# A fused attention and routing kernel on one core: new start, new ending, and three sets of transposes moved from TensorE to the DMA queues

## The chip, the core and the metric

The kernel runs on one core of one Trainium2 chip. A core has five instruction streams that run side by side and meet only at semaphores: PE (TensorE, the matrix multiplier, which writes to PSUM), ACT (ScalarE), DVE (VectorE), POOL (GpSimd) and SP (SyncE, which here only issues DMAs). Each stream executes its instructions strictly in the order in which they were written. The metric is the device time of one execution in microseconds; lower is better. Three runs of the kernel before are given, and one execution was recorded by the profiler.

## The reference, cut to what matters

The input is 2048 tokens of 512 bf16 values. They are normalized (xn), then two branches read xn, and their outputs are added to x.

```python
xn = layernorm(x)
# branch A: 32 heads of 16, four segments of 512 tokens, per segment s:
q, k, v = heads(xn @ wq), heads(xn @ wk), heads(xn @ wv)
phi = lambda t: where(t > 0, t + 1, exp(t))
a_dot = softmax(qs @ ks.T * scale + causal_mask) @ vs
a_mem = (phi(qs) @ M) / (phi(qs) @ z + 1e-6)          # M, z from earlier segments
o     = g * a_mem + (1 - g) * a_dot                   # g = sigmoid(beta)
M, z  = M + phi(ks).T @ vs, z + phi(ks).sum(0)
A = o @ wo
# branch B: one token is chosen and sent through a gated MLP
r = xn @ w_r;  t = argmax(r)
y = (silu(xn[t] @ w_gate) * (xn[t] @ w_up)) @ w_down * sigmoid(r[t])
B = xn, with y added to row t
out = x + A + B
```

Three things must be transposed on the way, since a matrix product on PE contracts over the partitions: xn (tokens on partitions, needed with channels on partitions), phi(K) (needed with tokens on partitions for `phi(ks).T @ vs`) and the attention output O (tokens on partitions, needed with channels on partitions for `o @ wo`).

## The kernel before

All work is cut into operations that are put on record through `Plan.op`: an engine, an assumed duration, what it reads and writes, and a due time `d`. `Plan.run` (L75) then simulates the engines with these durations and writes the instructions in the order that this gives: of the operations that could start, the one with the earliest due time goes first. The order on every engine is thus fixed when the program is built. The due times, and a field `e` before which the planner doesn't place an operation, exist only in the planner: on the chip an instruction starts when its engine reaches it and its semaphores are there.

The main loop is over 16 groups n: segment s = n // 4 and eight heads j = n % 4 of it. Each group has two units of four heads, and each unit five tiles of causal attention scores, so there are 160 tiles. A tile (`tile`, L426) is: PE computes scores into a PSUM buffer `st` (L436), ACT takes their exponential into `pt` (L439), POOL zeroes the part above the diagonal (L448), and PE multiplies with V into the accumulator `acc` (L457, 8 small products). There are two `st` buffers, two `acc` buffers and two further PSUM buffers, called `misc`, for everything else that PE computes. After the five tiles DVE divides by the row sums (L422, L423) and writes `Oseg`.

Around the tiles, PE has other work that the planner puts in between:

- the projections of K, Q and V (L358, L400), 512 columns each product;
- `ln` for the tokens of the next segment: DVE takes the statistics (L305), POOL normalizes (L321), PE transposes four 128x128 blocks into `misc` (L331), and DVE copies them to `xnT` (L334);
- `phi` (L366 to L369) of K and, from segment 1 on, of Q;
- `memT` (L463): PE transposes phi(K), four blocks at a time (L469), and DVE copies them to `pk` (L471); `memM` multiplies with V (L482), and `mem` applies the memory of earlier segments to phi(Q) (L505, L509), after which POOL adds the result to `Oseg` (L520);
- `fin` (L537), once for each block of 128 tokens: PE transposes four blocks of `Oseg` (L545), DVE copies them to `oT` (L547), PE adds a row block `rb` made by POOL (L525) and the product with `wo` (L550, L552), DVE adds x times a scale (L532), SP stores the block;
- `oT3` (L555): the same transposes for the last segment, kept in a buffer of their own;
- `moe` (branch B) and `guard` (a check of the norms of wq and wk, L574 to L598, whose result decides at L962 whether a slow path is run; it isn't run with these inputs).

SP issues all transfers, in the planned order: the loads, eight small DMAs for each group that place Q's heads into the zeroed buffers `QZ` (`scatter`, L373), and the stores. A DMA takes one of eight semaphores in turn, and waits until the DMA that had it before has landed.

The start: SP loads four blocks of x, then wk, wq, wv; PE runs 14 products on zeros; POOL clears `QZ` and sets `Vaug`'s ones; DVE normalizes four blocks; PE transposes them; K and Q of group 0 are projected from all four blocks at once, and four heads of `QZ` are written straight from PSUM by DVE and ACT (L811, L813). The ending (L850 to L880): the final products of four token blocks are started in two `misc` buffers and one `st` buffer (L859, L861), the last eight heads' part is transposed on PE together with the memory part (L866, L867), multiplied (L875), and DVE makes the four output blocks in turn (L878), which SP stores.

## Time and profile before

| what | value |
|---|---|
| median of 3 runs (lowest, highest) | 231.29 us (229.43, 232.02) |
| the profiled execution | 231.71 us |
| its span, first to last instruction | 230.0 us |
| mean granted TensorE clock | 0.95 |
| busy: PE, ACT, DVE, POOL | 204.0, 172.3, 158.2, 151.7 us |
| DMAs of Q's heads, count and size | 124 of 16 KB |

The profile is a recording of one execution. Its span is 1.71 us shorter than the time of that execution, which also counts what lies outside the first and last instruction. A busy time is the union of an engine's instructions; for PE, where the end of a product is modelled, it is better to compare the starts of neighbouring rows.

### The profile page before, as it was taken

Reading aid. Unit: us, or ns where it says so; the run is one execution under the profiler, and the core shown is the slowest. Engines: PE = TensorE matmul, PEld = TensorE weight load, DVE = VectorE, ACT = ScalarE, POOL = GpSimd, SP = SyncE. Lnnn points to the kernel's source line nnn. Section 1 sums busy time; section 2 is a strip of 40 time slices with the busy share of each in tenths; the row PEclk is TensorE's granted clock in tenths of the full one; section 3 lists DMA queues with packets and bytes.
Section 4 is the critical chain, followed back from the end, with each engine's and each line's share of the span. In section 5 each row is a group of like instructions: output and inputs, shape, how many; then the busy total and the mean of one; then the engine's idle time right before and its main releaser. Section 6 shows DMA issues by size and latency. Waiting matters only on the chain.

```text
span 230.0 us, 6827 instructions
## 1 busy us (share of the span) xinstructions
PE 204.0 (89%) x2680; PEld 133.5 (58%) x2717; DVE 158.2 (69%) x392; ACT 172.3 (75%) x203; POOL 151.7 (66%) x252
## 2 busy tenths in 40 slices
PE   7386999989999999989999999999989999998720
PEld 2143656656677677755677666556557767676410
DVE  6966999664776964554677977897787966583060
ACT  3127899999988968987687879968567998889300
POOL 8802487976965664847477689999627578868400
PEclk9769999999999988988999999999999999999965
DMA  5800597031000012660000010010100001110020
GB/s 172 273 13 7 155 297 261 24 102 23 4 6 22 3 27 58 234 215 12 14 4 24 24 43 29 30 44 26 46 1 28 20 17 36 36 37 26 0 95 15
DMA packets 15195, 14.39 MB, mean 63 GB/s; under 512 B 3184, under 2 KB 15152, under 8 KB 15152
## 3 DMA queue, kind: packets, MB, share of 16 engines
q1 hardware_dynamic: 15152, 13.85, 19.5%
q8 instruction: 23, 0.38, 0.7%
q14 instruction: 20, 0.16, 0.2%
HBM read 9.71 MB, written 2.10 MB: 51 GB/s over the span
## 4 chain that ended last, share of the span: by engine, by line
PE 55%; DVE 20%; ACT 7%; issue 5%; DMA 5%; POOL 4%; SPq 1%; POOLq 0%; ACTq 0%
PE st L436 19%; PE misc L358 9%; PE acc L457 8%; ACT pt L439 6%; PE misc L552 4%; PE misc L400 4%; DVE bnst L305 3%; DMA x_all<-in_A_x_dram 3%; POOL pt L448 2%; DMA QZ<-raw_q 2%; DVE KT L390 2%; DVE Oseg L423 1%; PE misc L550 1%; DVE ob L532 1%; PE misc L331 1%
## 5 line engine op out<-in xcount | busy, mean ns | idle before, releaser
L439 ACT ACTIVATE pt<-st 128x1024 bf16<-128x1024 f32 x160 | 155.2, 1025 | 30.3 <-PE st L436 24.5
L448 POOL TENSOR_SCALAR_AFFINE_SELECT pt<-pt 128x512 bf16<-128x512 bf16 (+1 forms) x160 | 88.1, 556 | 54.0 <-ACT pt L439 51.4
L436 PE MATMUL st<-QZ,KT 128*128 128x512 bf16 (+3 forms) x507 | 95.8, 302 | 3.3 <-DVE QZ L811 1.2
L457 PEld LDWEIGHTS <-pt 128*128 128x128 bf16 x1280 | 50.0, 96 | 22.7 <-POOL pt L448 6.5
L457 PE MATMUL acc<-Vaug,pt 128*128 128x17 bf16 x1280 | 53.5, 171 | 2.8 <-POOL pt L448 1.5
L436 PEld LDWEIGHTS <-KT 128*128 128x128 bf16 x512 | 39.1, 98 | 17.1 <-issue 5.8
L358 PE MATMUL misc<-xnT,wk 128*128 128x512 bf16 x57 | 18.4, 406 | 1.2 <-ACT xnT L336 0.7
L367 POOL TENSOR_SCALAR am<-ex 128x512 bf16<-128x512 bf16 x24 | 14.9, 622 | 6.8 <-ACT ex L366 6.2
L358 PE MATMUL misc<-xnT,wq 128*128 128x512 bf16 x55 | 17.3, 395 | 0.5 <-issue 0.2
L400 PE MATMUL misc<-wv,xnT 128*128 128x512 bf16 x58 | 16.6, 378 | 1.0 <-DVE raw_q L815 0.6
L520 POOL TENSOR_TENSOR Oseg<-Oseg,om 128x512 bf16<-128x512 bf16 x11 | 13.4, 1219 | 3.5 <-DVE om L515 2.1
L532 DVE SCALAR_TENSOR_TENSOR ob<-x_all,s,misc 128x512 bf16<-128x512 bf16 x12 | 9.0, 747 | 9.2 <-PE misc L552 9.0
L422 DVE RECIPROCAL rr<-acc 128x16 f32<-128x16 f32 x32 | 7.9, 247 | 9.8 <-PE acc L457 9.8
L402 DVE TENSOR_TENSOR Vaug<-misc,omg_bc 128x512 bf16<-128x512 f32 x16 | 11.0, 689 | 4.6 <-PE misc L400 4.3
L423 DVE TENSOR_TENSOR Oseg<-acc,rr 128x256 bf16<-128x256 f32 x32 | 13.5, 423 | 0.9
L379 DVE CAST raw_q<-misc 128x512 bf16<-128x512 f32 x15 | 10.3, 688 | 5.5 <-PE misc L358 3.0
L525 POOL TENSOR_SCALAR rb<-ybc,onehot,cvec 128x512 bf16<-128x512 bf16 x16 | 12.3, 771 | 0.8 <-DVE rm L511 0.3
L390 DVE CAST KT<-misc 128x512 bf16<-128x512 f32 x15 | 10.3, 687 | 3.5 <-PE misc L358 2.8
L305 DVE BATCH_NORM_STATS2 bnst<-x_all 128x6 f32<-128x512 bf16 x16 | 10.7, 670 | 0.9 <-DMA x_all<-in_A_x_dram 0.9
L552 PE MATMUL misc<-wo,oT 128*128 128x512 bf16 x40 | 10.7, 378 | 0.4
L331 PE MATMUL misc<-ident,xn 128*128 128x128 bf16 x64 | 6.8, 240 | 4.3 <-DVE xn L321 2.9
L358 PEld LDWEIGHTS <-wk 128*128 128x128 bf16 x64 | 6.0, 100 | 6.2 <-issue 1.8
(154 smaller groups left out, 258.4 us busy)
## 6 DMA issues: line engine op xcount, KB each, us to landing
out_dram<-ob SPq DMA_DIRECT2D x16, 128.0 KB, 1.8
QZ<-raw_q SPq DMA_DIRECT2D x124, 16.0 KB, 1.8
mw<-in_B_w_gate_dram SPq DMA_DIRECT2D x2, 896.0 KB, 7.0
mw<-in_B_w_up_dram SPq DMA_DIRECT2D x2, 896.0 KB, 6.6
mw<-in_B_w_down_dram SPq DMA_DIRECT2D x2, 896.0 KB, 5.9
x_all<-in_A_x_dram SPq DMA_DIRECT2D x3, 512.0 KB, 4.4
x_all<-in_A_x_dram SPq DMA_DIRECT2D x4, 128.0 KB, 2.2
wk<-in_A_wk_dram SPq DMA_DIRECT2D x1, 512.0 KB, 4.2
```

The lines of the kernel that those rows point to most:

```text
L305: pl.op("DVE", .61, lambda: nc.vector.bn_stats(out=st[:], in_=x_all[:, b, :]), r=[("x", b)], w=[st], d=d)
L358: self.pl.op("PE", .216, lambda cb=cb: nc.tensor.matmul(ps[:], lhsT=w[:, cb, j * P:(j + 1) * P], rhs=xnT[:, cb, s * L:(s + 1) * L], start= ...
L367: pl.op("POOL", .58, lambda: nc.gpsimd.tensor_scalar(out=am[:], in0=ex[:], scalar1=1.0, scalar2=0.0, op0=ALU.min, op1=ALU.max), r=[ex], w= ...
L390: o = self.pl.op("DVE", .61, lambda: nc.vector.tensor_copy(out=kt[:], in_=ps[:]), r=[ps], w=[kt], d=d + 1)
L400: self.pl.op("PE", .216, lambda cb=cb: nc.tensor.matmul(ps[:], lhsT=xnT[:, cb, b * P:(b + 1) * P], rhs=wv[:, cb, :], start=(cb == 0), stop ...
L423: pl.op("DVE", .345, lambda: nc.vector.tensor_tensor(out=Oseg[s][:, j, :, 4 * w:4 * w + 4, :], in0=av()[:, :, :, 0:DH], in1=rr[:, :, :, No ...
L436: nc.tensor.matmul(st[:, i, off:off + n], lhsT=lh, rhs=QZ[q][:, h, q0:q0 + n], start=True, stop=True)
L439: pl.op("ACT", .907, lambda: nc.scalar.activation(out=pt[:], in_=st[:], func=ACT.Exp, scale=SCALE), r=[st], w=[pt], d=d)
L448: nc.gpsimd.affine_select(out=mv, in_=mv, pattern=pat, compare_op=ALU.is_ge, fill=0.0, base=0, channel_multiplier=-1)
L457: nc.tensor.matmul(acc[:, q0 // P + c, i, e, :], lhsT=pt[:, i, off + c * P:off + (c + 1) * P], rhs=Vaug[:, 4 * s + kb, h, :], start=first, ...
L520: pl.op("POOL", 1.12, lambda: nc.gpsimd.tensor_tensor(out=Oseg[s][:, j], in0=Oseg[s][:, j], in1=om[:], op=ALU.add), r=[om], w=[("O", s, j, ...
L552: pl.op("PE", .216, lambda cb=cb: nc.tensor.matmul(fin[:], lhsT=oT[:, cb, :], rhs=wo[:, cb, :], start=False, stop=(cb == NCB - 1)), r=[oT, ...
```

## The change

The change has four parts.

**Transposes by DMA.** The transposes of xn for segments 1 to 3 (12), of phi(K) (12, now cut by heads j and not by token block) and of O (12 in `fin`, 4 in `oT3`) become `dma_start(..., transpose=True)` on SP's queue, 128x512 bf16 each (128x256 in `oT3`). They write SBUF, so the `misc` buffer and DVE's copy go away. `Oseg` is laid out by token block first, so that a block's 512 columns are contiguous.

**The start.** x's blocks 1 and 3 and wk are loaded from ACT's queue. POOL's and DVE's clearing is put in another order, constants that are used late are set later, 22 products on zeros are spread among the transposes, the projections of group 0 go block by block, K is copied by ACT, and all four heads of `QZ` come from the bf16 copy `raw0`. The four transposes of the first segment stay on PE.

**The ending.** O's transposes for the heads j = 2 and 3 of the last segment stay on PE and take the memory part with them (`late`). Two of the four final blocks get x times its scale from PE, through three bf16 diagonal matrices whose sum is the scale to f32 precision (L904 of the changed kernel), and go out through ACT, copy and DMA.

**The planner.** Scores, exponentials and the products with V are kept in the order of the tiles; an operation of DVE that is marked `lock` is planned at times at which POOL is idle; `moe` is due 5 earlier and its small products are spread out; `guard` multiplies the other way round, so that each sum has one column and not 512.

```diff
         def ln_T(self, b, xb, eng, d):
             pl = self.pl
+            if eng == "DMA":
+                pl.op("SP", .5, lambda: nc.sync.dma_start(out=xnT[:, :, b * P:(b + 1) * P], in_=xb[:], transpose=True), r=[xb], w=[("xnT", b)], d=d, lat=DTL)
+                return
...
-            self.pl.op("PE", .226, mm, r=[("pkT", s, j) for j in range(NCB)], uses=[src], w=[tp], d=d)
-            o = self.pl.op("DVE", .33, lambda: nc.vector.tensor_copy(out=pk[:, tb, :], in_=tp[:].rearrange("p j c -> p (j c)")), r=[tp], w=[("pk", s, tb)], uses=[pk], d=d + .5)
+            self.pl.op("SP", .5, lambda: nc.sync.dma_start(out=pk[:, :, j * P:(j + 1) * P], in_=src[:, j, :], transpose=True), r=[("pkT", s, j)], w=[("pk", s, j)], uses=[src, pk], d=d, lat=DTL)
...
-            pl.op("PE", .226, mm, r=[("O", s, j, w) for j in range(NCB) for w in range(2)], w=[ops], d=d)
-            o = pl.op("DVE", .33, lambda: nc.vector.tensor_copy(out=oT[:], in_=ops[:]), r=[ops], w=[oT], d=d + .5)
+            pl.op("SP", .5, lambda: nc.sync.dma_start(out=oT[:], in_=Oseg[s][:, qb].rearrange("p c a b -> p (c a b)"), transpose=True), r=[("O", s, j, w) for j in range(NCB) for w in range(2)], w=[oT], d=d - 2, lat=DTL)
...
-                    pl.op("PE", .216, lambda sq=sq, ps=ps: nc.tensor.matmul(ps[:], lhsT=ones_colb[:], rhs=sq[:], start=True, stop=True), r=[sq], w=[ps], d=dd + 1)
+                        for j in range(NCB):
+                            nc.tensor.matmul(ps[:, j:j + 1], lhsT=sq[:, j * P:(j + 1) * P], rhs=ones_colb[:], start=True, stop=True)
...
+    for b in (0, 2):
+        ld("SP", [("x", b)], x_all[:, b, :], x_d[:, b, :], .1 * b, 2.1)
+        ld("ACT", [("x", b + 1)], x_all[:, b + 1, :], x_d[:, b + 1, :], .1 * b, 2.1)
+    ld("SP", ["wq"], wq[:], wap(A_wq), 1.0, 4.5)
+    ld("ACT", ["wk"], wk[:], wap(A_wk), 1.1, 4.5)
...
+            for tb in range(4):
+                for t, w, wkey, dd in ((psq, wq, "wq", 8.0), (ps, wk, "wk", 8.1)):
...
+            pl.op("DVE", .61, lambda: nc.vector.tensor_copy(out=raw0[:], in_=psq[:]), r=[psq], w=[raw0], d=8.5)
+            pl.op("ACT", .6, lambda: nc.scalar.copy(out=kt0[:], in_=ps[:, 0, :]), r=[ps], w=[kt0], d=9)
+            for i, h in enumerate((0, 2, 1, 3)):
+                pl.op("DVE", .22, lambda h=h: nc.vector.tensor_scalar(out=QZ[0][:, h, :], in0=raw0[:], scalar1=bdsel[:, h:h + 1], scalar2=None, op0=ALU.mult), r=[raw0], w=[("QZ", 0, h)], d=9 + .1 * i, lock=True)
...
+            pl.op("DVE", 1.0, diag, r=[("s1", bb), "cpool"], w=dg + [res], d=td(150), lock=True)
+            for i in range(3):
+                pl.op("PE", .216, lambda t=t, i=i, dg=dg, bb=bb, sub=sub: nc.tensor.matmul(sub(t), lhsT=dg[i][:], rhs=x_all[:, bb, :], start=False, stop=False), r=[dg[i]], w=[key], uses=[t], d=dd)
...
-        pl.op("SP", .5, lambda b=b, tt=tt: nc.sync.dma_start(out=out_d[:, b, :], in_=tt[:]), r=[tt], d=td(165))
+        if qb >= 2:
+            pl.op("DVE", .66, lambda b=b, t=t, tt=tt, sub=sub: nc.vector.scalar_tensor_tensor(out=tt[:], in0=x_all[:, b, :], scalar=s1[:, b:b + 1], in1=sub(t), op0=ALU.mult, op1=ALU.add),
+                  r=[key, ("s1", b)], w=[tt], uses=[t], d=td(164))
+        else:
+            pl.op("ACT", .6, lambda t=t, tt=tt, sub=sub: nc.scalar.copy(out=tt[:], in_=sub(t)), r=[key], w=[tt], uses=[t], d=td(164))
+        eng = "SP" if qb >= 2 else "ACT"
```

How it moves instructions, at three places. The first is POOL's row from the late constants on to the first work of group 0, before (`QZ_145` and `QZ_146` are the two Q buffers, `sq` belongs to `guard`, `am` to phi):

```order
L255 IOTA tokidx 128x16
L770 MEMSET QZ_145 128x1024
L774 MEMSET Vaug 128x128
L772 MEMSET QZ_146 128x1024 x4
L774 MEMSET Vaug 128x128 x3
L574 TENSOR_TENSOR sq<-wq 128x512 x2
L367 TENSOR_SCALAR am<-ex 128x512
L448 AFFINE_SELECT pt<-pt 128x2x128
```

and now, where the Q buffers are `QZ_136` and `QZ_137`:

```order
L776 MEMSET QZ_136 128x1024
L234 AFFINE_SELECT bdsel<-bdsel 128x8
L778 MEMSET Vaug 128x128
L776 MEMSET QZ_137 128x1024
L454 AFFINE_SELECT pt<-pt 128x2x128
L776 MEMSET QZ_137 128x1024
L454 AFFINE_SELECT pt<-pt 128x2x256
L454 AFFINE_SELECT pt<-pt 128x4x128
```

Before, nine clearings and two squarings stood ahead of everything that waits for another engine; now the masks of the first tiles come after four clearings (one more of `QZ_136` stands a few rows above), and the rest is spread among them.

The second is SP's row in the third segment, where the stores of segment 1 go out, before:

```order
L534 DMA out_dram<-ob 128x512 x2
L373 DMA QZ_145<-raw_q 16x512 x8
L534 DMA out_dram<-ob 128x512 x2
L373 DMA QZ_146<-raw_q 16x512 x8
L534 DMA out_dram<-ob 128x512 x2
```

and now (`Oseg_141` is segment 1's output, `pkT` is phi(K)):

```order
L541 DMA_TRANSPOSE oT<-Oseg_141 128x4x128 x2
L533 DMA out_dram<-ob 128x512
L379 DMA QZ_136<-raw_q 16x512 x5
L471 DMA_TRANSPOSE pk<-pkT 128x4x128
L379 DMA QZ_136<-raw_q 16x512 x3
L471 DMA_TRANSPOSE pk<-pkT 128x4x128
L533 DMA out_dram<-ob 128x512
L471 DMA_TRANSPOSE pk<-pkT 128x4x128
L533 DMA out_dram<-ob 128x512
L541 DMA_TRANSPOSE oT<-Oseg_142 128x4x128 x2
L379 DMA QZ_137<-raw_q 16x512 x8
```

The transposes stand between the eight DMAs of a group and ahead of those of the next.

The third is PE's row at the last tile, before (`st<-wo,oT_153` belongs to the final products in the `st` buffer, `st<-QZ_146,KT` is the last tile's score):

```order
L861 LDWEIGHTS oT_153
L861 MATMUL st<-wo,oT_153 128x512
L436 LDWEIGHTS KT
L436 MATMUL st<-QZ_146,KT 128x512
L436 LDWEIGHTS KT
L436 MATMUL st<-QZ_146,KT 128x512
L457 LDWEIGHTS pt
L457 MATMUL acc<-Vaug,pt 128x17
```

and now, behind the 24 products with V that follow that score:

```order
L463 LDWEIGHTS pt
L463 MATMUL acc<-Vaug,pt 128x17
L890 LDWEIGHTS ident
L890 MATMUL st<-rb,ident 128x512
L906 LDWEIGHTS oT_144
L906 MATMUL st<-wo,oT_144 128x512
```

The final products that use the `st` buffer stood ahead of the last tile's score, and now stand behind it.

More of the change, by code (lines that the diff above doesn't have):

```diff
@@ L146, in run @@
             free[e] = end
+            if o["lock"]:
+                port[0] = end
             fin = end + o["lat"]
@@ L261, in build_kernel @@
     xnT = big.tile([P, NCB, S], bf16, name="xnT")
-    Oseg = [big.tile([P, NCB, 4, 8, DH], bf16, name=f"Oseg{s}") for s in range(NSEG)]
+    Oseg = [big.tile([P, 4, NCB, 8, DH], bf16, name=f"Oseg{s}") for s in range(NSEG)]
     oT3 = big.tile([P, 4, NCB, P], bf16, name="oT3")
@@ L599, in guard @@
-            pl.op("DVE", .5, last, r=[("fs", 0), ("fs", 1)], w=["nbad"], d=d + 28)
+                            nc.vector.tensor_tensor(out=sqs[:, i, :], in0=sqs[:, i, :], in1=ps[:], op=ALU.add)
+                    self.misc.append(pl.op("DVE", .1, acc, r=[ps, ("sqs", i)], w=[("sqs", i)], d=dd + 2))
+            nbad_i = small_t["nbad"] = stat.tile([1, 1], i32, name="nbad_i")
+            hs, bad, cnt = stat.tile([8, 2, NCB], f32, name="hs"), stat.tile([8, 3], f32, name="bad"), self.ps([1, 1])
@@ L847, in build_kernel, with late, mm @@
     pl.op("SP", .3, values, r=["nbad"], d=td(152), e=td(120))
+    def late(j, ts, d):
+        for hb in range(2):
+            for qb in (2 * hb, 2 * hb + 1):
+                def mm(hb=hb, qb=qb):
+                    nc.tensor.matmul(ts[hb][:, qb % 2, :], lhsT=Oseg[3][:, qb, j].rearrange("p a b -> p (a b)"), rhs=ident[:], start=True, stop=False)
+                    nc.tensor.matmul(ts[hb][:, qb % 2, :], lhsT=B.om_late[j][:, qb].rearrange("p a b -> p (a b)"), rhs=ident[:], start=False, stop=True)
+                pl.op("PE", .115, mm, r=[("O", 3, j, 0), ("O", 3, j, 1), B.om_late[j]], w=[ts[hb]], d=d)
+            if hb == 0 or j == 2:
+                o = pl.op("DVE", .3, lambda hb=hb: nc.vector.tensor_copy(out=oT3[:, 2 * hb:2 * hb + 2, j, :], in_=ts[hb][:]), r=[ts[hb]], w=[("oT3l", j, hb)], d=d)
+            else:
+                o = pl.op("ACT", .35, lambda hb=hb: nc.scalar.copy(out=oT3[:, 2 * hb:2 * hb + 2, j, :], in_=ts[hb][:]), r=[ts[hb]], w=[("oT3l", j, hb)], d=d)
+            if j == 2:
+                B.misc.append(o)
+    late(2, [B.ps([P, 2, P]) for i in range(2)], td(152.5))
     busy = list(B.misc)
```

304 lines of the change are left out of this document (151 added, 153 removed).

## The prediction

> **What bounds the kernel now.** I read the busy time by stretches first, then who waits for whom, then PE's own rows in order of time, then the start and the ending. The first view has, for each stretch, its length and the busy time of PE, PE's weight loads, DVE, ACT and POOL with the number of instructions, then granted clock and DMA share:
>
> ```profile
> 19.60:60.00 40.40, 38.05 (x487) 24.48 (x494) 31.25 (x76) 38.49 (x49) 29.47 (x50) 1.00 0.40 124
> 60.00:100.00 40.00, 39.26 (x690) 28.59 (x696) 26.73 (x84) 34.67 (x41) 26.01 (x44) 0.96 0.20 60
> 100.00:140.00 40.00, 38.51 (x510) 25.81 (x517) 28.94 (x71) 31.17 (x37) 27.41 (x45) 0.96 0.14 43
> 140.00:180.00 40.00, 38.15 (x441) 23.83 (x448) 31.46 (x68) 29.88 (x34) 31.09 (x47) 1.00 0.09 26
> 180.00:213.00 33.00, 31.91 (x454) 22.41 (x459) 22.09 (x56) 30.32 (x34) 24.53 (x42) 1.00 0.10 29
> ACT pt L439 <- PE st L436: 24.5, 30, 3.4
> ```
>
> The first tiles are bound by ACT (38.5 of 40.4 us). From 60 us on ACT is busy for 126 of 153 us and PE for 147.8. The last row says whom ACT waits for: PE's scores, 24.5 us in all. So from 60 us on the sum of PE's work sets the pace. That PE has work without a gap, and isn't just shown busy, is read from its starts:
>
> ```profile
> 138.77 0.38 PE L575 MATMUL misc<-sq,ones_colb 128*1 128x512 bf16 x1
> 139.08 0.40 PE L545 MATMUL misc<-ident,Oseg 128*128 128x128 bf16 x4
> 139.32 1.18 PE L436 MATMUL st<-QZ,KT 128*128 128x512 bf16 x4
> 92.22 0.84 PE L695 MATMUL misc<-xselT,mw 128*128 128x1 bf16 x28
> 92.92 0.59 PE L436 MATMUL st<-QZ,KT 128*128 128x512 bf16 x2
> ```
>
> Each row starts where the one ahead of it lets go: four transposes (L545) take 0.24 us of PE, one product of `guard` 0.31, and 28 products of one column 0.70, or 0.025 each.
>
> **The start.** In order of time (start, duration, engine, line; in brackets the idle time before and what ended it):
>
> ```profile
> 0.80 1.28 ACT L221 ACT_TABLE_LOAD   x1 [0.80 <-PEq L1002]
> 0.80 2.10 DMA x_all<-in_A_x_dram
> 2.92 0.69 DVE L305 BATCH_NORM_STATS2 bnst<-x_all 128x6 f32<-128x512 bf16 x1 [0.76 <-DMA x_all<-in_A_x_dram]
> 3.23 3.93 POOL L772 MEMSET QZ<- 128x1024 bf16 x4
> 6.11 0.18 DVE L306 BATCH_NORM_AGGREGATE MV<-bnst 128x2 f32<-128x6 f32 x1
> 6.21 3.80 DVE L321 TENSOR_SCALAR xn<-x_all,rstd,cvec 128x512 bf16<-128x512 bf16 x2
> 9.92 0.99 DVE L315 SCALAR_TENSOR_TENSOR cvec<-MV,rstd 128x2 f32<-128x2 f32 x1
> 10.71 0.59 ACT L336 COPY xnT<-misc 128x512 bf16<-128x512 bf16 x1 [3.85 <-PE misc L331]
> 10.95 0.41 DVE L321 TENSOR_SCALAR xn<-x_all,rstd,cvec 128x512 bf16<-128x512 bf16 x1
> 11.75 1.01 PE L331 MATMUL misc<-ident,xn 128*128 128x128 bf16 x8 [1.08 <-DVE xnT L334]
> 13.28 0.23 ACT L790 ACTIVATE eb<-bcl 128x32 f32<-128x32 f32 x1
> 13.44 1.86 PE L358 MATMUL misc<-xnT,wk 128*128 128x512 bf16 x4 [0.67 <-ACT xnT L336]
> 15.34 0.69 DVE L807 CAST KT<-misc 128x512 bf16<-128x512 f32 x1 [0.96 <-PE misc L358]
> 16.06 0.29 DVE L368 TENSOR_SCALAR tp<-KT 128x512 bf16<-128x512 bf16 x1
> 19.52 1.01 ACT L439 ACTIVATE pt<-st 128x1024 bf16<-128x1024 f32 x1
> ```
>
> Two normalizations (L321) take 3.80 us while POOL clears and squares, and each of the two later ones 0.41. So 3.0 us go there, and most of 0.99 on the small L315 behind them. Then K's four products take 1.86 us, over twice their pace later on. The first exponential (L439) starts at 19.52.
>
> After the change POOL has done its four clearings before the normalizations come, and then stops at the first mask. I rebuild the path from these rows. Block 1 of x, behind the table load on ACT's queue, lands at 2.08 + 2.10 = 4.2. Three more statistics, 0.69 and 0.18 (L306) each, end at 6.8; two normalizations, the small L315 and two more at 0.41 end at 8.6. DVE copies the first transposed block by 9.0, the last two blocks can then go through PE (8 transposes in 1.0) to 10.0, the copy out takes 0.6 (ACT's row), and the last block's products with wq and wk some 0.5, to 11.1. Then the cast (0.69) and four writes of `QZ` at 0.29 in 2-byte SBUF, 13.0; and since ACT's order has the small exponential of beta, which waits for DVE behind the `QZ` writes, ahead of the first tile, 0.23 (L790) and as much on DVE: 13.4. Some ten hand-overs of up to 0.1 us make it 14.4. That is 5.1 us earlier. The bounds: 6.1 without hand-overs, 3.5 if PE still runs at half pace there. All work of the loop moves with it, since x's later blocks stand behind these steps in SP's queue.
>
> **The loop.** What goes away on PE after 60 us, by the groups and the one stretch of L331 (its length, busy time, count):
>
> ```profile
> L469 PE MATMUL misc<-ident,pkT 128*128 128x128 bf16 x48 | 4.5, 218 | 0.0
> L545 PE MATMUL misc<-ident,Oseg 128*128 128x128 bf16 x48 | 4.6, 218 | 0.2 <-DVE Mrun L487 0.2
> L560 PE MATMUL misc<-ident,Oseg 128*128 128x128 bf16 x12 | 1.2, 218 | 0.0
> 60.00:100.00 40.00, 1.15 (x12) 0.96 0.20 60
> L575 PE MATMUL misc<-sq,ones_colb 128*1 128x512 bf16 x8 | 3.0, 377 | 0.0
> ```
>
> 48 + 48 + 12 + 12 products in blocks of four are 30 blocks, at 0.24 us 7.2 us. Of these, 8 transposing products come back for heads j = 2 (0.4). `guard` loses 8 x 0.31 = 2.5 and gets 32 x 0.025 = 0.8. Sum 8.5 us. ACT's idle time in the four stretches (5.3, 8.8, 10.1, 2.7 us) is larger than what each loses (about 1.7, 2.3, 3.2, 1.7, by where the blocks and `guard` lie), so all of it counts. Before 60 us another 9 blocks (2.2 us) go, but there ACT has only 1.9 us of slack: I take 0.7. DVE loses some 39 copies of 0.41 and POOL nothing; both are off the path, and I credit 1.0 us for PE's waits for a free `misc` buffer, out of the 5.2 us in which PE is idle in the four stretches. The planner's new order and the spread of branch B change no engine's sum, and I count them as nothing: what covers them is that PE is never without work from 60 us on.
>
> What comes in its place is 40 transposing DMAs on SP's queue. No row shows one. The nearest are these (start and time of SP's issuing; then size and time to landing):
>
> ```profile
> 132.65 4.95 SPq L373 DMA_DIRECT2D QZ<-raw_q  x8
> 221.08 2.31 SPq L880 DMA_DIRECT2D out_dram<-ob  x4
> out_dram<-ob SPq DMA_DIRECT2D x16, 128.0 KB, 1.8
> x_all<-in_A_x_dram SPq DMA_DIRECT2D x3, 512.0 KB, 4.4
> wr_col<-in_B_w_r_dram SPq DMA_DIRECT2D x1, 1.0 KB, 8.1
> ```
>
> An issue takes 0.6 us (4.95 / 8; 2.31 / 4), the same 128 KB land in 1.8 us (and in 2.1 at the start), 512 KB in 4.4, and a transfer cut into 2-byte pieces in 8.1 (behind three large loads). So one transposition lands in 1.8 to 8.1 us; I take 2 to 3, by the rows of the same size. Are there consumers that would wait? xn for the next segment is made some ten tiles or more ahead. `oT` has two buffers, so a block's transposition is issued when the block two before is multiplied, about ten tiles ahead. phi(K)'s last eight heads are the tightest, with some five tiles, 6 us. So up to about 5 us the landing is hidden. What isn't is SP's queue: Q's heads stand behind transposes that wait for POOL, DVE or a free `oT`, and PE's scores wait for Q's heads. I take 1.0 us for it, with bounds 0 and 6 (0.5 us in 12 of the 15 groups).
>
> The Trainium skill, "Advanced Engine Details and Errata", section X-Bar Transpose (TRN2), says that a transposing DMA is as fast as a regular one; by that the 1.0 stands. "VectorE: DVE Perf Modes", section The three transpose paths, has 1309 ns for 128x128 by DMA against 390 on TensorE, and advises TensorE: four blocks would be an estimated 5.2 us each, at the edge of what is hidden. The trace puts PE's own price far below that page's, 0.06 us for a block in a stream, and no run here shows the DMA's; if the page holds and the transfers follow one another, the second rival below is what happens.
>
> **The ending:**
>
> ```profile
> 214.89 0.81 PE L861 MATMUL st<-wo,oT 128*128 128x512 bf16 x3
> 215.54 0.59 PE L436 MATMUL st<-QZ,KT 128*128 128x512 bf16 x2
> 216.23 1.02 ACT L439 ACTIVATE pt<-st 128x1024 bf16<-128x1024 f32 x1 [2.43 <-PE st L436]
> 221.63 1.40 DVE L878 SCALAR_TENSOR_TENSOR ob<-x_all,s,st 128x512 bf16<-128x512 bf16 x2
> ```
>
> The last score (L436) stands behind the final products (L861), and ACT is idle for 2.43 us until it comes. With the score ahead of them that goes: 2.4. The last two of DVE's four output blocks end the row; two blocks go to ACT, beside it: 1.4. The late transposes and six diagonal products at 0.22 (L861, three in 0.65) add 1.3 to a PE that is full there; half of it is hidden behind the last mask: 0.6. Net 3.2, bounds 1 and 4.
>
> **The sum.** 230.0 - 5.1 (start) - 8.5 - 0.7 - 1.0 (loop) + 1.0 (SP) - 3.2 (ending) = 212.5 us of span. With the 1.7 us around it this is 214.2 for the profiled execution, which stood 0.4 above the median; so 213.8, rounded to 214.
>
> **Rivals.**
>
> First, PE's relief doesn't reach the end, because ACT's scores now wait for Q's heads behind the transposes in SP's queue, in place of PE. For it: 0.9 DMAs per tile stand in that queue already, at 0.6 us each. Against it: before, PE waited for them in one visible place only. Then start and ending alone count: 230.0 - 5.1 - 3.2 + 1.7 - 0.4 = 223.
>
> Second, a transposition holds SP's queue or the DMA engines while it runs. SP has about 155 other DMAs at 0.6, 93 us. 40 transposes fit into the rest of some 195 us of loop up to 2.6 us each, and eat all gains at about 3.0 (18 us more over 40). Priced by the row of 4.4 us for 512 KB it is 93 + 176 = 269 us, and slower than before. The row of 8.1 us speaks for it, those of 1.8 and 2.1 against it.
>
> Third, the loop gets down to what ACT needs. ACT's busy time from 19.6 to 213 is 164.5 us; with the start's 14.4 and an ending of 13 it would be 192. PE's busy time there, 185.9 less 10.7, is larger: 14.4 + 175.2 + 13 + 1.7, some 204 to 206.
>
> **How the numbers follow.** The forecast has 0.66 (its own range 208 to 219), the first rival 0.18 (219 to 226), the second 0.09, the third 0.07 (below 208). The range of 207 to 224 leaves out the second rival, a part of the third and the upper end of the first, under 2 in 10. About 1% is what a measurement of this kernel can tell from no change; that is 229.0 to 233.6. Faster: forecast, third, and nearly all of the first, 0.89. Slower: 0.08. Within 1%: 0.03.
>
> **What would show it.** The start is right if the first exponential begins near 14.4, and its mechanism if all four L321 on DVE take 0.41. The loop is right if the stretch from first to last tile is 10 us shorter and PE still has no gaps; it is wrong if PE or ACT wait for Q's heads or for `xnT`, `pk`, `oT`. The DMA estimate is right if the transposes land in 2 to 3 us, and the second rival is what happens if SP's rows for them are 3.0 us or longer. The ending is right if the idle time of 2.43 us ahead of the last exponential is gone and DVE makes two blocks. If the landing is above 5 us, the prediction is wrong by the waits that this brings.

## The result, and the profile after

| what | before | changed |
|---|---|---|
| median (runs) | 230.52 us (4) | 223.52 us (4) |
| ratio of times, 95% interval | | 0.967 [0.9575, 0.9764] |
| the profiled execution, its span | 231.71, 230.0 us | 223.13, 221.4 us |
| mean granted clock in it | 0.95 | 0.97 |
| busy: PE, ACT, DVE, POOL | 204.0, 172.3, 158.2, 151.7 | 197.2, 171.5, 135.6, 149.3 us |

The change makes the kernel 7 us faster; 17 were forecast. Executions of one kernel differ by up to some 5 us here: medians below are over all runs, ratios leave the slowest executions out, where the two disagree the ratio is used, and the executions recorded for e1, e2, e11 and e13 are among the slowest of their kernels.

The timeline of the changed kernel at its start and its ending (start, duration, engine and line; in brackets the idle time ahead and what ended it):

```profile
6.81 0.71 DVE L324 TENSOR_SCALAR xn<-x_all,rstd,cvec 128x512 bf16<-128x512 bf16 x2
...
7.69 0.74 DVE L324 TENSOR_SCALAR xn<-x_all,rstd,cvec 128x512 bf16<-128x512 bf16 x2
...
14.53 2.83 ACT L445 ACTIVATE pt<-st 128x1024 bf16<-128x1024 f32 x3
...
210.00 1.02 ACT L445 ACTIVATE pt<-st 128x1024 bf16<-128x1024 f32 x1 [1.35 <-PE st L442]
...
214.80 1.41 DVE L914 SCALAR_TENSOR_TENSOR ob<-x_all,s,st 128x512 bf16<-128x512 bf16 x2 [1.13 <-PE st L910]
```

The first exponential starts at 14.53 (before: 19.52), the last at 210.00 (216.23). From the last one to the end of the span it is 11.4 us, where it was 13.8. So start and ending gave what they were to give, and the loop between the two exponentials, 196.7 us before, still takes 195.5. What is missing, 8.9 us of span (221.4 for the 212.5 forecast), is in the loop. Its stretches, with the columns and the bounds of the table in the prediction:

```profile
19.60:60.00 40.40, 34.73 (x433) 21.47 (x432) 24.85 (x61) 33.40 (x43) 30.51 (x54) 0.96 0.54 138
60.00:100.00 40.00, 35.20 (x638) 25.56 (x637) 22.84 (x74) 33.32 (x41) 25.41 (x43) 0.91 0.47 96
100.00:140.00 40.00, 38.94 (x546) 25.39 (x544) 27.80 (x77) 34.31 (x40) 29.98 (x49) 1.00 0.23 60
140.00:180.00 40.00, 38.33 (x493) 24.60 (x492) 28.08 (x76) 32.23 (x37) 31.47 (x50) 1.00 0.26 57
```

In the first two, PE (second number) is idle for 5.7 and 4.8 us, where it had been idle for 2.4 and 0.7, and the granted clock has dropped to 0.96 and 0.91. In the last two ACT does more per stretch than before (34.31 and 32.23 against 31.17 and 29.88): there the relief of PE works. Who stops PE, in all, times and longest:

```profile
PE misc L618 <- DMA xnT<-xn: 3.3, 2, 2.3
PE misc L364 <- DMA xnT<-xn: 2.9, 1, 2.9
PE misc L406 <- DMA xnT<-xn: 2.5, 1, 2.5
PE misc L481 <- DMA pk<-pkT: 1.5, 2, 0.9
...
PE st L442 <- DMA QZ<-raw_q: 0.8, 2, 0.6
```

It is the transposed x, in the projections of the second segment (L406, L364) and in the router (L618), not Q's heads. The transposing DMAs beside the plain ones, with the median from issue to landing:

```profile
out_dram<-ob SPq DMA_DIRECT2D x14, 128.0 KB, 2.5
...
oT<-Oseg SPq DMA_TRANSPOSE x16, 2.7
...
xnT<-xn SPq DMA_TRANSPOSE x12, 2.5
pk<-pkT SPq DMA_TRANSPOSE x12, 2.4
```

So a transposition as such isn't slow. What makes PE stop these four times is in a timeline of POOL's normalization, SP's issues and PE's products:

```profile
25.50 0.51 SPq L610 DMA_DIRECT2D mw<-in_B_w_up_dram  x1
...
26.66 3.14 SPq L331 DMA_TRANSPOSE xnT<-xn  x1
...
31.55 0.77 POOL L324 TENSOR_SCALAR xn<-x_all,rstd,cvec 128x512 bf16<-128x512 bf16 x1
...
35.34 0.61 PE L406 MATMUL misc<-wv,xnT 128*128 128x512 bf16 x1 [2.48 <-DMA xnT<-xn]
...
36.00 1.01 PE L442 MATMUL st<-QZ,KT 128*128 128x128 bf16 x4
...
38.94 1.80 SPq L379 DMA_DIRECT2D QZ<-raw_q  x3
...
40.83 1.22 SPq L331 DMA_TRANSPOSE xnT<-xn  x1
...
43.34 0.60 PE L364 MATMUL misc<-xnT,wq 128*128 128x512 bf16 x2 [2.86 <-DMA xnT<-xn]
43.78 0.60 PE L442 MATMUL st<-QZ,KT 128*128 128x256 bf16 x4
...
73.59 0.27 PE L618 MATMUL misc<-wr_col,xnT 128*128 128x1 bf16 x4 [2.31 <-DMA xnT<-xn]
```

Two different delays are seen. The segment's first transposition is issued at 26.66 behind 896 KB loads, holds SP for 3.14 us and lands at 35.3, 8.6 us after its issue. The segment's fourth is ready to go at 32.3, when POOL has written xn (31.55 + 0.77), but SP issues it at 40.83: for 8.5 us two other transpositions, at 1.2 us of SP each, and Q's heads at 0.6 stood ahead of it. (One of the two was itself held up for 0.5 us by a late load, by SP's own list of waits.) Then it lands within 2.5 us. The first stop costs more than its length: the four scores at 36.00, of 128 columns each, take 1.01 us, and those at 43.78, of 256 columns and at full clock, 0.60. The stop at 43 us, though the longest, has no slow clock behind it. Windows of 2 us (PE's busy time second, clock third from the end), and the granted clock in 40 slices of 5.5 us of the changed kernel:

```profile
36.00:38.00 2.00, 2.00 (x13) 0.93 (x11) 0.00 (x0) 0.89 (x1) 0.00 (x0) 0.50 0.21 46
44.00:46.00 2.00, 2.00 (x29) 1.38 (x27) 0.99 (x3) 1.53 (x3) 0.43 (x1) 1.00 0.13 31
```

```profile
PEclk9999996999999589999999999999999999999998
```

The 6 is the slice of the stop at 35 us, 5 and 8 are those of the router's stops and what follows.

### The profile page after: what moved, and what is told of

It reads as the page before. It is cut to its first block, busy times and chain, and to the rows that moved or that the text cites. A ratio compares the mean times of both kernels' runs of the same rounds, so it can differ in the third digit from the quotient of the medians.

```text
span 221.4 us, 6740 instructions
## 1 busy us (share of the span) xinstructions
PE 197.2 (89%) x2635; PEld 126.5 (57%) x2635; DVE 135.6 (61%) x367; ACT 171.5 (77%) x204; POOL 149.3 (67%) x250
## 4 chain that ended last, share of the span: by engine, by line
PE 62%; DMA 12%; ACT 8%; DVE 6%; POOL 4%; issue 3%; SPq 2%; ACTq 0%; DVEq 0%
PE st L442 25%; PE acc L463 10%; PE misc L364 8%; ACT pt L445 7%; DMA xnT<-xn 6%; PE misc L406 6%; PE misc L545 4%; DMA wk<-in_A_wk_dram 4%; POOL pt L454 2%; SPq L379 1%; PE misc L543 1%; DMA pk<-pkT 1%; PE misc L508 1%; POOL Oseg L519 1%; DMA QZ<-raw_q 1%
## 5 line engine op out<-in xcount | busy, mean ns | idle before, releaser
L454 POOL TENSOR_SCALAR_AFFINE_SELECT pt<-pt 128x512 bf16<-128x512 bf16 (+1 forms) x160 | 88.7, 561 | 54.0 <-ACT pt L445 53.1
L442 PE MATMUL st<-QZ,KT 128*128 128x256 bf16 (+3 forms) x512 | 97.4, 304 | 1.7 <-DMA QZ<-raw_q 0.8
L463 PE MATMUL acc<-Vaug,pt 128*128 128x17 bf16 x1280 | 52.3, 171 | 0.9 <-POOL pt L454 0.4
L442 PEld LDWEIGHTS <-KT 128*128 128x128 bf16 x512 | 39.8, 98 | 19.6 <-issue 3.8
L406 PE MATMUL misc<-wv,xnT 128*128 128x512 bf16 x64 | 18.9, 389 | 2.5 <-DMA xnT<-xn 2.5
L364 PE MATMUL misc<-xnT,wq 128*128 128x512 bf16 x60 | 17.2, 378 | 2.9 <-DMA xnT<-xn 2.9
L364 PE MATMUL misc<-xnT,wk 128*128 128x512 bf16 x60 | 17.2, 382 | 0.0
L545 PE MATMUL misc<-wo,oT 128*128 128x512 bf16 x48 | 13.3, 378 | 0.0
L519 POOL TENSOR_TENSOR Oseg<-Oseg,om 128x512 bf16<-128x512 bf16 x10 | 11.7, 1171 | 1.3 <-DVE om L514 0.8
L514 DVE TENSOR_TENSOR om<-misc,rm 128x512 bf16<-128x512 f32 x12 | 8.3, 689 | 3.9 <-PE misc L508 3.7
L406 PEld LDWEIGHTS <-xnT 128*128 128x128 bf16 x64 | 5.9, 99 | 7.8 <-DMA xnT<-xn 2.9
```

What stands on the lines that cost most here:

```text
L364: self.pl.op("PE", .216, lambda cb=cb: nc.tensor.matmul(ps[:], lhsT=w[:, cb, j * P:(j + 1) * P], rhs=xnT[:, cb, s * L:(s + 1) * L], start= ...
L406: self.pl.op("PE", .216, lambda cb=cb: nc.tensor.matmul(ps[:], lhsT=xnT[:, cb, b * P:(b + 1) * P], rhs=wv[:, cb, :], start=(cb == 0), stop ...
L442: nc.tensor.matmul(st[:, i, off:off + n], lhsT=lh, rhs=QZ[q][:, h, q0:q0 + n], start=True, stop=True)
L454: nc.gpsimd.affine_select(out=mv, in_=mv, pattern=pat, compare_op=ALU.is_ge, fill=0.0, base=0, channel_multiplier=-1)
L463: nc.tensor.matmul(acc[:, q0 // P + c, i, e, :], lhsT=pt[:, i, off + c * P:off + (c + 1) * P], rhs=Vaug[:, 4 * s + kb, h, :], start=first, ...
L519: pl.op("POOL", 1.12, lambda: nc.gpsimd.tensor_tensor(out=Oseg[s][:, :, j], in0=Oseg[s][:, :, j], in1=om[:], op=ALU.add), r=[om], w=[("O", ...
```

## The experiments

Theory A: the loss is PE's stops on late xnT. Its rivals are named with each run. Every ratio is to runs of the kernel before on the same chip.

**Which transposes lose.** `e1_xnT_pe` gives x's transposes back to PE (its edit is shown), `e3_all_pe` those of phi(K) and O as well:

```diff
-                self.ln_T(b, xb, "DMA", d + 2 + sp * i)
+                self.ln_T(b, xb, "DVE", d + 2 + sp * i)
```

> The transposes of xn for segments 1 to 3 go back to PE with DVE's copy; phi(K) and O stay on DMA. Theory A (late xnT: in the changed kernel PE stood in front of products whose xnT had not landed, 8.6 us between 32 and 74 us, and ran at a lower clock behind each such stop): these stops go, PE gets 12 blocks (2.9 us) back, 10 to 11 us of stop and slow clock less 2.9 us, of which half is hidden where ACT is the bound: 215.5 us, range 213 to 218, no stretch with a granted clock of 0.6 after 20 us. Theory B (the new order of the planner, not the DMAs, made the loop slow): 223 to 226. Theory C (the rest of the loop did not profit from PE's relief at all): the 60th exponential comes as early as in the kernel before less 5 us, and the time is 222 to 225.

> New start, new ending and new planner, and all transposes on PE with DVE's copies: no transposing DMA is left. Splits the change. Theory A (transposes by DMA give 8.5 us of PE time back in the later two thirds and lose about as much or more by late xnT in the first third): no stops, but the loop from 60 us on as long as before: 219.5 us, range 216 to 223. If the DMAs were a clear net gain: 226 to 231. If start and ending were all that helped and order did nothing: 222.

Measured: 215.48 us, 0.9297 [0.9223, 0.9372], and 219.39 us, 0.9469 [0.9397, 0.9541]. Both came out at theory A's times. With x on PE the kernel is the fastest of all in this order: phi(K) and O by DMA gain 3.9 us, x by DMA loses 8.0. e1's list of stops (PE's longest, without those of the start) has no transposition left:

```profile
PE misc L481 <- DVE gmin L650: 1.5, 1, 1.5
...
PE st L442 <- DMA QZ<-raw_q: 0.4, 2, 0.2
```

One thing that theory A expected did not come: the granted clock of e1's recorded execution still falls, to 0.50 from 72 to 82 us, behind the stop of 1.5 us on `gmin`, which is part of the routed branch and no transposition.

**Is it the large loads?** `e2_mw_late` plans the first three loads of the MLP's weights at 40 us or later:

```diff
-                pl.op("SP", .5, go, w=[t], d=dd, e=min(dd, 16.0), lat=6.0)
+                pl.op("SP", .5, go, w=[t], d=dd, e=max(min(dd, 16.0), 40.0), lat=6.0)
```

> As the changed kernel, but the first three weight loads of branch B (896 KB each) are planned no earlier than 40, so that they are issued behind the transposes of xn for segment 1. Theory A1 (the first transpose was late, 8.6 us, because its packets stood behind these loads): it lands in 2.4 to 3 us, the stop at 33 to 35 us and the slow clock behind it go, and SP's queue doesn't fall behind, so the stop at 40 to 43 us goes too or halves: 218.5 us, range 216 to 221. Theory A2 (SP's 1.2 us for each transpose is what makes them late, the loads don't matter): the stop at 33 us shrinks and that at 41 us stays, 221 to 224.

Measured: 223.09 us, 0.9638 [0.9569, 0.9706]. The stop on the first block is gone, that on the fourth (L364) stays, as the rival A2 had it, and the time is the rival's too:

```profile
PE misc L481 <- DMA pk<-pkT: 4.5, 1, 4.5
PE misc L364 <- DMA xnT<-xn: 3.0, 1, 3.0
PE st L442 <- DMA QZ<-raw_q: 2.8, 3, 2.1
```

The loads do make a transposition late: the first block, with no load ahead of it, lands 2.5 us after its issue, and the block that is issued behind the loads, at 51.51, 10.2 us after its own. But the loads now stand ahead of phi(K)'s transpositions, and PE stops for those, 4.5 us.

**Is it the planner's wrong numbers?** `e4_issue` has it count 1.22 us of SP for a transposition and a landing 1.7 us behind that (shown for x; phi(K) and O are changed alike):

```diff
-    DTL = 2.4
+    DTL = 1.7
...
-                pl.op("SP", .5, lambda: nc.sync.dma_start(out=xnT[:, :, b * P:(b + 1) * P], in_=xb[:], transpose=True), r=[xb], w=[("xnT", b)], d=d, lat=DTL)
+                pl.op("SP", 1.22, lambda: nc.sync.dma_start(out=xnT[:, :, b * P:(b + 1) * P], in_=xb[:], transpose=True), r=[xb], w=[("xnT", b)], d=d, lat=DTL)
```

> As the changed kernel, but the planner counts 1.22 us of SP for a transposing DMA, as the trace shows, and not 0.5, and lets it land 1.7 us after that (2.9 in all, as before). Only the order changes. Theory A2 (the queue of SP is what the planner misjudged): fewer and shorter stops before xnT, 217 to 221. Theory A1 (the loads ahead of the first transpose): the stop at 33 us stays, 221 to 224.

Measured: 221.92 us, 0.9627 [0.9553, 0.9701]: PE still stops for xnT, 2.3, 1.9 and 1.7 us in all at its three places, and the time lies where the rival had it (221 to 224). At most a small part.

**Only the segment that stops.** `e5_seg1_pe` transposes the second segment's x on PE and leaves eight blocks to the DMA; `e6_seg1_pe_moe45` also plans the routed part five tiles later:

```diff
+                self.ln_T(b, xb, "DVE" if g in {1} else "DMA", d + 2 + sp * i)
...
-            B.moe(td(40))
+            B.moe(td(45))
```

> The changed kernel, but the normalized x of the second segment (four of the twelve blocks) is transposed by PE, and the other eight by DMA. Theory A (the loss of the xnT part, 8.0 us between 223.5 with it and 215.5 without, is the stops of PE in front of late xnT blocks and not a price of each transposition): the two stops at 35.3 and 43.3 us (2.5 and 2.9 us) go and with them some 1 us of matmuls at half clock, against 4 x 0.24 = 1.0 us of new PE work; the router's stops at 71 to 73 us (3.3 us in all) stay: about 218.5 us. Theory B (each of the twelve transpositions costs the same 0.67 us by holding SP and the DMA engines): 4 x 0.67 = 2.7 us come back, 220.8 us, and the DMA waits of PE on xnT move to other blocks.

> As the run before it, and the routed part with its router (which reads all of xnT) is planned five tiles later. Theory A: the router's two stops for xnT (1.0 and 2.3 us) go too, so that no stop of PE on xnT over 1 us is left, about 215.5 us, as with all twelve blocks on PE, though eight of them are still made by DMA. Theory B: nothing more comes back than with the second segment alone, 220.8 us.

Measured: 225.81 us, 0.9747 [0.9668, 0.9827], and 221.62 us, 0.9576 [0.9505, 0.9647]. Both theories miss with the first. The stops on xnT did go, all but 0.8 us, as A had it, but its conclusion that the time comes back with them falls. In e5's timeline:

```profile
52.06 0.51 DVE L375 TENSOR_TENSOR pkT<-tp,am 128x512 bf16<-128x512 bf16 x1
...
53.08 1.23 SPq L471 DMA_TRANSPOSE pk<-pkT  x1
...
57.65 1.22 SPq L331 DMA_TRANSPOSE xnT<-xn  x1
...
58.95 2.39 SPq L471 DMA_TRANSPOSE pk<-pkT  x1
...
62.63 0.41 PE L481 MATMUL misc<-Vaug,pk 128*128 128x136 bf16 x4 [2.90 <-DMA pk<-pkT]
```

and in e1's, with no xnT in SP's queue:

```profile
46.78 1.32 SPq L471 DMA_TRANSPOSE pk<-pkT  x1
...
49.82 4.23 SPq L471 DMA_TRANSPOSE pk<-pkT  x3
```

With x on PE, phi(K)'s four transpositions are issued from 46.8 to 54.0. In e5 they go out between 53.1 and 61.3, the last one 6.4 us behind the DVE row that writes its input, and PE stops 2.9 us for it. x's blocks for the third and fourth segment, which no projection needs yet, stand ahead of it. One more thing differs: in the planner's order PE comes to the first of these products at 56.5 in e5 and at 66.7 in e1. So the stop moves to whatever is late next in the queue, and the order decides how early it is wanted. With e6 theory A misses again (215.5). It comes near B's number, but with e5's stops on phi(K) (2.7 us the longest), not with an equal price of each transposition: with four transpositions less, e5 gains nothing. Where e5's own time goes isn't accounted for in full.

**Is the queue or are the DMA engines full?** `e12_act_queue` issues x's transposes from ACT:

```diff
-                pl.op("SP", .5, lambda: nc.sync.dma_start(out=xnT[:, :, b * P:(b + 1) * P], in_=xb[:], transpose=True), r=[xb], w=[("xnT", b)], d=d, lat=DTL)
+                pl.op("ACT", 1.22, lambda: nc.scalar.dma_start(out=xnT[:, :, b * P:(b + 1) * P], in_=xb[:], transpose=True), r=[xb], w=[("xnT", b)], d=d, lat=DTL)
```

> The changed kernel, but the twelve transposing DMAs of normalized x are issued by ACT on its own queue, counted as 1.22 us each by the planner. Queue theory (xnT and phi(K) are late because loads, transpositions and scatters stand in one queue of SP): xnT lands 2.5 us behind its issue also behind the large loads, phi(K) is no longer late, PE's stops on transposes go; ACT has 12 x 1.2 = 14.6 us of issues more in the loop and is 173 us busy of 221, so some of that is paid as late exponentials: 216 to 220 us. Rival (the DMA engines, not the queue, are what the transpositions wait for): the first transposition lands 8 us after its issue all the same, and with the issues on ACT the time is 225 us or more.

Measured: 237.13 us, 1.0322 [1.0238, 1.0407]. The rival holds for the first block: alone in its queue it is issued at 27.30 and PE gets it at 35.1, as late as on SP's queue.

```profile
27.30 1.30 ACTq L331 DMA_TRANSPOSE xnT<-xn  x1
...
35.14 0.60 PE L406 MATMUL misc<-wv,xnT 128*128 128x512 bf16 x2 [3.33 <-DMA xnT<-xn]
```

So behind the large loads a queue of its own doesn't help a transposition: from 26 to 34 us, while the loads land, the 16 DMA engines are shown as full in this run (a busy share of 1.06 to 1.14). What a later block waits for ahead of its issue (the 8.5 us above) is SP's queue. Stops of PE's products on phi(K) are gone in this run, but scores now wait 8.1 us in all for exponentials: ACT must wait for xn before it issues, and stands still meanwhile.

**What the clock costs.** `e9_fill` leaves the order as it is and puts products of zeros where PE stops (one of four places):

```diff
+                if b == 4 and cb == 0:
+                    self.fill(ps[:], 10)
+                nc.tensor.matmul(ps[:], lhsT=xnT[:, cb, b * P:(b + 1) * P], rhs=wv[:, cb, :], start=(cb == 0), stop=(cb == NCB - 1))
```

> The changed kernel, the order of its work untouched, with matmuls of zeros put in front of the four matmuls at which PE stops for xnT (10 and 11 of 128x512 ahead of those at 35.3 and 43.3 us, 8 and 20 of 128x256 ahead of the router's last two blocks), into accumulators that the next matmul overwrites: PE waits as long as before but is not idle. They use 0.22 us each for 128x512, so they fit into the stops of 2.5, 2.9, 1.0 and 2.3 us. Clock theory (a stop also halves the granted clock behind it, and this is half of the loss): the slices at .6, .5 and .8 in the row of the granted clock go to full, which are 0.4 + 0.5 + 0.2 of a slice of 5.5 us, some 6 us of PE time: 217.5 us. Rival (the half clock is no cost, since what PE loses there it makes good, or it is not set off by the stops): 223.5 us, or up to 2 us more for the zeros.

Measured: 221.22 us, 0.9634 [0.9561, 0.9706]. The clock stays full up to the last slice, the waits remain:

```profile
PEclk9999999999999999999999999999999999999995
```

The time is 2.3 us lower by the medians and 0.8 us by the ratios (0.967 and 0.9634), which can't be told from nothing; the theory had 6. With products in place of most of the idle time the drop doesn't come, so in this kernel it was PE's idleness at the stops that set it off. What the drop cost stays open between nothing and a few us.

**Another order of SP's queue.** `e13_late_seg1pe` has the second segment's x on PE, as e5, plans x of the third and fourth segment some 30 tiles later and the routed part at tile 64; `e14_late_allpe` is the same with x all on PE. Of e13's edit, the later places:

```diff
-    LNAT = {1: (1, 4, 2.0), 2: (2, 14, 2.0), 3: (3, 26, 2.0)}
+    LNAT = {1: (1, 4, 2.0), 2: (2, 44, 2.0), 3: (3, 54, 2.0)}
...
-            B.moe(td(40))
+            B.moe(td(64))
```

> The changed kernel with the second segment's x transposed by PE, the normalization and the transposing DMAs of the third and fourth segment planned 30 tiles later (at tiles 44 and 54 instead of 14 and 26; they are used from tiles 72 and 112 on) and the routed part, which reads all of xnT, at tile 64 instead of 40. On SP's queue three of the four transpositions of phi(K) of the first segment now stand ahead of all of these xnT. Order theory: phi(K) is issued as its blocks are made (46 to 54 us, as in the first experiment), no stop of PE on pk or xnT over 1 us is left, and the time comes to that of the kernel with x all on PE, 215 us. Rival (the eight transpositions of x cost the time by themselves, in any order): 220 us or more, with new stops where they now stand, or slower scores for QZ scatters that wait behind them.

> As the run before it, but x all transposed by PE: the control of what the later places do alone. Order theory: the same as the run before it, plus 8 x 0.24 = 1.9 us of PE work: 215 to 217. Rival: 215, and 5 us or more below the run before it.

Measured: 223.37 us, 0.9705 [0.9646, 0.9763], and 220.59 us, 0.9593 [0.9544, 0.9642]. The order theory falls: there is no order tried here in which x by DMA costs nothing. Eight blocks cost 2.8 us. Stops of e13:

```profile
PE misc L545 <- DMA oT<-Oseg: 2.9, 3, 1.4
...
PE misc L618 <- DMA xnT<-xn: 2.1, 2, 1.7
...
PE misc L481 <- DMA pk<-pkT: 1.1, 1, 1.1
```

and of e14:

```profile
PE misc L545 <- DMA oT<-Oseg: 2.9, 2, 2.3
```

The stops on `oT` stand in both, so they don't belong to x by DMA; what x by DMA adds are those on xnT and pk, 3.2 us. The later places by themselves cost 5 us (220.6 against e1's 215.5, which has no stop on `oT`); whether these stops are the reason wasn't tried.

**The same kinds in a second order.** `e10_e1_moe44` and the last four plan the routed part four tiles later; `e7_only_oT` and `e8_only_pk` give phi(K) or O back to PE in addition to x, and `e11_e1_issue` has e1 with e4's numbers.

> The changed kernel with the transposes of normalized x and of phi(K) on PE, and only those of O by DMA. The three kernels measured so far put the two DMA parts that are left (phi(K) and O) at 219.4 - 215.5 = 3.9 us together. By the count of blocks on PE after the first segment (12 of phi(K), 16 of O, 0.24 us each) O's part is worth about 2.2 us: 217.2. Rival: phi(K)'s part brings nothing or a loss, since its heads are needed soon after they are made: 215.5 or less. Other rival: O's part brings nothing as its transposes stand in the gaps of late tiles: 219.4.

> The changed kernel with the transposes of normalized x and of O on PE, and only those of phi(K) by DMA. By the count of blocks phi(K)'s part is worth about 1.7 us: 217.7. Rival: it brings nothing or a loss, 219.4 or more, and PE waits for pk at the start of a memory sum. Other rival: it brings the whole of the 3.9 us: 215.5.

> The first experiment's kernel (x transposed by PE, phi(K) and O by DMA), with the routed part planned four tiles later. In its profile the only stop of PE over 1 us in the loop is one of 1.5 us behind the router, and the granted clock is 0.76 from 74 to 94 us behind it. Clock theory: the place of the router moves, and if the stop gets shorter the clock stays at full there, 0.24 x 20 = 4.8 us of PE time: 213 us in all runs. Rival: the order does not matter there, 215.5.

> The first experiment's kernel, and the planner counts the transposing DMAs as measured: 1.22 us of SP each and a landing 1.7 us behind it, where it had 0.5 and 2.4. With the x part gone, SP's queue has few stops to remove: 215.5 us, within 1.5 us. Rival: the remaining waits on pk and QZ cost something and go: 213.

> The changed kernel with the routed part planned four tiles later. Kind theory (transposing x by DMA costs 8 us in this kernel, by stops of PE on xnT or on what stands behind xnT in SP's queue, wherever the router is): 223 us against the 215.2 of the kernel with x on PE and the same place, and the profile shows over 5 us of PE's waits for xnT, pk and QZ together. Order theory (the 8 us belong to one order): 219 or less.

> All transposes on PE, the routed part four tiles later. Kind theory: 4 us above the kernel with phi(K) and O by DMA at the same place, 219 us. Order theory: anything from 215 to 222.

> Only O by DMA, the routed part four tiles later. If phi(K)'s part is worth 3.9 us, as 219.4 against 215.5 had it: 219. By the count of PE blocks (1.7 us): 217. Order theory: anything from 215 to 222.

> Only phi(K) by DMA, the routed part four tiles later. If O's part is worth the 4 us and more that the first pair had: 219 to 221. By the count of PE blocks (2.2 us): 217.4. Order theory: anything from 215 to 222.

| by DMA | routed part at 40: median, ratio | at 44: median, ratio |
|---|---|---|
| x, phi(K), O | 223.52, 0.967 [0.9575, 0.9764] | 227.04, 0.9845 [0.9767, 0.9923] |
| phi(K), O | 215.48, 0.9297 [0.9223, 0.9372] | 215.18, 0.9324 [0.9259, 0.9389] |
| none | 219.39, 0.9469 [0.9397, 0.9541] | 222.23, 0.9672 [0.9622, 0.9722] |
| O | 219.42, 0.9525 [0.9453, 0.9596] | 221.16, 0.9642 [0.9583, 0.9700] |
| phi(K) | 221.76, 0.9547 [0.9438, 0.9656] | 216.89, 0.9426 [0.9373, 0.9480] |

e11 took 218.49 us, 0.9392 [0.9319, 0.9465]: the right numbers gain nothing there. In both orders x by DMA loses (by the medians 8.0 and 11.9 us) and phi(K) with O gains (3.9 and 7.1). x's sign is the same in a third order, that of e13 and e14 (eight blocks). An order by itself moves the time by 3 to 5 us (e14 against e1, e15 against the changed kernel), so that the sizes belong partly to the order; that the signs belong to the kind of transposition is borne out by three orders for x, and only by two for phi(K) and O. For phi(K) or O alone the runs settle nothing: alone, phi(K) gives no gain that can be told in the first order and 5 us in the second, O none in either. Several expectations missed. e7 and e8 came out where O alone, and phi(K) alone, bring nothing. e10 has its rival's 215.5: another place of the router brings nothing. e11 is 3 us above what was expected. e15 is slower than both theories had it, though with the stops that the kind theory named; e16 and e17 are 2 to 3 us above the kind theory's 219, and e18 lies within 1 us of the count of PE's blocks. In the second order the changed kernel stops as in the first:

```profile
PE st L442 <- DMA QZ<-raw_q: 3.9, 4, 1.9
PE misc L364 <- DMA xnT<-xn: 2.9, 1, 2.9
PE misc L618 <- DMA xnT<-xn: 2.5, 1, 2.5
PE misc L406 <- DMA xnT<-xn: 2.4, 1, 2.4
```

The best kernels found are e1 and e10, at 215.5 and 215.2 us, 7% below the kernel before.

## Why the prediction was wrong, point by point

- **Start, -5.1:** right. The first exponential came at 14.53 for 14.4, and four normalizations on DVE take 1.45 us for 1.64. wk landed 9.0 us after its issue and PE stopped 0.9 us for it, a step that the prediction's path doesn't have, so that others must have been shorter.
- **Ending, -3.2:** right in sum. The hole of 2.43 us shrank to 1.35, it didn't vanish; from the last exponential to the end it is 2.4 us less. Together 3.5.
- **PE's relief in the loop, -8.5 - 0.7 - 1.0:** right in mechanism, and no longer to be split exactly, since the planner's order alone moves the time by 3 to 5 us. e1 leaves x's share out (12 blocks, about 1.4 us of this sum) and comes to 215.5, where the prediction's terms without x's share give 215.2. That the two agree so well is in part luck: phi(K) and O by DMA gained 3.9 us (7.1 in the other order), where the sum has 6.1 for their 27 blocks less the eight products that come back, and e3, without any of the DMAs, is 1.9 us faster than start, ending and `guard` alone would make it (221.3), with a new order that the sum counted as nothing.
- **The +1.0 for SP's queue, bounds 0 and 6, is the step that failed.** It rested on "up to about 5 us the landing is hidden" and on xn being "made some ten tiles or more ahead". The landing was foreseen (2 to 3 us; 2.4 to 2.7 measured). But the time to hide was counted from landing alone. The fourth block's xn was ready at 32.3 and PE came to its product at 40.5 (43.34 less the stop): 8.2 us, all of which went by in SP's queue ahead of the issue. An issue takes 1.2 us of SP, not 0.6, and the transposition sits in the queue at the place at which the planner, with 0.5 us for each, believed that there was room; telling the planner the right time (e4) shortened the stops only a little. The term measured as x's transposes by DMA against PE is a loss of 8.0 us in this order and 11.9 in the other, net of what PE is relieved of; those of phi(K) and O do pay.
- **What stood behind large loads** was in the prediction as an end of the range (8.1 us to landing, `wr_col`), and taken for unlikely. It is what happened to the first block: 8.6 us.
- **The rivals.** The first gave 223 us, and that is the time, but by luck: its mechanism, scores that wait for Q's heads, is 0.8 us in the profile, and PE's relief did reach ACT from 100 us on. In its place stands a stop of PE on xnT, with the same queue as its cause. The second needed 3.0 us a transposition in SP's rows; they are 1.2, and four blocks land in 2.4 to 2.7 us, not in the 5.2 of the prediction's estimate. The statement of the Trainium skill in "Advanced Engine Details and Errata", section X-Bar Transpose (TRN2), that a transposing DMA is as fast as a regular one, agrees with the landings here (2.4 to 2.7 us beside 2.5 for 128 KB). The issue took 1.2 us beside 0.6.
- **The sum counted no price for a stop beyond its length.** The granted clock falls behind the stop at 35 us and those of the router; what that cost is 0.8 to 2.3 us by e9, not clear of noise.

What stays open: how much of each difference is one order's chance, and whether any order exists in which x by DMA gains.

## What to carry to other kernels

What this case teaches: a transfer that replaces work on an engine is hidden only if its place in the issuing queue comes early enough: count from the moment its input is ready, through everything that stands ahead of it in the queue, to its landing, and compare with the consumer's place in its own engine's order. Move to the DMA first those transposes whose consumers are far away (O and phi(K) here), and leave on the matrix engine what is consumed soon or issued behind large loads. Where removing a stop doesn't bring its time back, look which transfer of the same queue is late next.

## What the runs showed of the hardware

A transposing DMA of 128x512 bf16 from SBUF to SBUF occupies the issuing queue for 1.2 us, on SP as on ACT, twice a plain DMA of 128 KB (0.6). Behind 896 KB loads it landed after 8.6 us, after 7.8 from a queue of its own (e12), and after 10.2 in e2.

The granted clock falls to about half for a few us also where PE hardly stops. In e10 it does so after 64 products of one column each (L675, from 75.81 on); the timeline of their larger part, and windows of 2 us with PE's busy time second and the clock third from the end:

```profile
77.08 1.14 PE L675 MATMUL misc<-onehot,x_all 128*128 128x1 bf16 x40
```

```profile
76.00:78.00 2.00, 1.72 (x62) 1.63 (x59) 1.88 (x7) 1.61 (x3) 1.14 (x1) 1.00 0.11 29
78.00:80.00 2.00, 1.95 (x45) 1.37 (x43) 0.73 (x3) 0.00 (x0) 1.66 (x4) 0.74 0.12 25
80.00:82.00 2.00, 2.00 (x27) 1.19 (x25) 1.84 (x5) 1.10 (x2) 0.61 (x1) 0.50 0.09 24
...
86.00:88.00 2.00, 2.00 (x43) 1.45 (x42) 1.90 (x5) 1.61 (x2) 1.56 (x2) 1.00 1.07 277
```

PE is shown busy for 1.72 us and more in each window, and is still at about half clock for some 6 us. No run tried this by itself, but the other traces narrow it down. Behind the same 64 products the clock falls also in the kernel before (0.55 from 84 us on), e12, e16, e17 and e18, where 32 to 60 of them stand in a row; it stays at 1.00 in e3, e7, e9 and e14, where at most 20 do, with other products between. One column alone doesn't do it: behind the router's 64 one-column products in a row (e12, from 94.46 on) the clock is 1.00. What sets the two apart stays open.

The Trainium skill, "TensorE: Matmul & The Clock Gate", Part 1, has the clock fall to half after an idle window of about 3.4 us. Here it fell behind stops of 2.5 us (at 35 us) and, in e1, of 1.5 us, and not behind one of 2.9 us (at 43 us), so that the length of a stop alone doesn't decide.
